# A spectral filter and an MLP on one core: the second DFT stage in quarters of the array, and VectorE's DFT operations spread over steps

## The chip, the cores and the metric

The kernel runs on one core of a Trainium2 chip. The metric is the device time of one execution in microseconds. Before the change three runs gave 776.87, 777.8 and 780.51, with a median of 777.8 us.

## What is computed

```python
X = np.fft.rfft(x, axis=1)                   # x: 8 x 3008 x 256
y = np.fft.irfft(X * (filt_r + 1j * filt_i), n=3008, axis=1)
h = y.reshape(24064, 256) @ w_in             # 256 x 2048
s = np.sin(alpha * h)
out = (h + s * s / (alpha + 1e-9)) @ w_out   # 2048 x 256
```

Eight batches pass through a Fourier filter along the sequence, and each of the 24064 rows through an MLP with a sine activation.

## The kernel before

**Two kinds of work share the engines.** The MLP is cut into 48 chunks (`chunks`, L588), twelve for each pair of batches, of 512 rows and one in twelve of 384; a chunk is eight *steps* (L749 to L760), so a batch is 48 steps. In each step `hidden` (L594) makes two blocks: two matmuls into a PSUM tile ph of the pool hps (L601), a cosine on ScalarE (L605), and on VectorE v, which reads the cosine and ph again (L606). `project` (L610) multiplies the v of the chunk before with w_out, eight matmuls a step (L620), and stores through ScalarE and a DMA queue. A ph tile is free once its v is made; hps has four buffers, so the blocks of a step reuse those of two steps ago.

**The DFT of the batches is slipped between the steps.** 3008 = 47 x 64. For a batch there are four stages, with a trip through DRAM after the first and after the third:
- first stage: 47 points over the columns. Batch 1 uses `first` (L203, 16 matmuls with the full table wf), later batches `first_tiled` (L214), whose eight matmuls per quarter of the batch use 64x64 quarters of the array: two row groups hold two different sets of x rows, two column groups two sets of n2. The results t1_h go to DRAM as d1 (L211, L229).
- second stage forward: `forward` (L238), 12 times a batch, two frequencies each, 128x128 tables d. `load_t2` (L233) reads d1 back on POOL's queue. ScalarE copies the PSUM to xf (L246), and two DMAs on SP's queue put its halves, exchanged, into xs.
- product with the filter: `product` (L253) multiplies xf into p, `cross` (L261) multiplies xs in place and adds it to p. xf and xs have three buffers, p seven.
- second stage inverse: `inverse` for batch 1 (L266), `inverse_tiled` later (L284): three bursts a batch of 16 quarter matmuls, evacuated into g by three ScalarE copies and one VectorE copy; g goes to DRAM as d2. `load_t4` and `last` (L316) finish into y, which the MLP reads.

Bursts use PSUM tiles of two pools: their first half (q = 0) takes the two of fps, their second half (q = 1) two of the four of hps, out of the same rotation as ph. Batch 0 has a path of its own ahead of the steps (L459 to L513).

**What sets the order.** Nothing is scheduled at run time: every engine works its instructions in the order in which the program issues them, and so do the DMA queues of SP and POOL. `put(at, fn)` (L671) gives each piece of the DFT a time in steps; `slot` (L735) issues the pieces due, once after the hidden blocks of a step and once after its projection. `firsts` and `inverses` (L674, L679) hold the times of the bursts; `clear` moves forwards off them, and `aside` (L689) moves a VectorE operation that would come just ahead of a burst to just behind it. `after` (L99) makes one instruction wait for another.

Of the kernel before, what the change touches and what calls it, by code (L numbers as in the profile page):

```python
# [24 lines left out]
FUSED = 1  # L25
TILED = 2


def dft_tables():
# [22 lines left out]
    f16 = np.float16  # L52
    wf, wi = wf.reshape(N1 * 2, 2, NS, 2), 2 * wi.reshape(2, NS, 2, NR)
# [13 lines left out]
    return (eh.astype(f16), wh.reshape(NK, NR).astype(f16), wt.reshape(128, 64).astype(f16), wf.transpose(0, 2, 1, 3).reshape(NR, NK).astype(f16), wi.reshape(NK, NR).astype(f16), d,  # L67
# [4 lines left out]
def kernel(  # L72
# [11 lines left out]
    eh_host, wh_host, wt_host, wf_host, wi_host, d_host, wf0_host, wi0_host, e_host = dft_tables()  # L84
# [3 lines left out]
    wf_dram = nc.inline_tensor(wf_host, name="wf_tbl")  # L88
    wi_dram = nc.inline_tensor(wi_host, name="wi_tbl")
# [20 lines left out]
    t2pool = pool("t2", 4)  # L110
    xfpool = pool("xf", 3)
    ppool = pool("pp", 7)
    xspool = pool("xs", 3)
# [8 lines left out]
    wf_t = cpool.tile([NR, NK], FP16)  # L122
# [22 lines left out]
    eh_t = e_t[:, 0:NS // 2].rearrange("p a (b m) -> p (a b) m", m=64)  # L145
# [3 lines left out]
    wi_t = cpool.tile([NK, NR], FP16)  # L149
    wi0_t = cpool.tile([128, NR], FP16)  # L150
    filt_t = cpool.tile([128, 2, NS, C], FP16)
    f_t = [filt_t[:, k] for k in range(2)]
# [3 lines left out]
    def load_x(b, ch):  # L156
        xt = xpool.tile([128, 8, C], FP16, name=f"x_{b}_{ch}", tag="x")
        if b >= TILED:
            for h in range(2):
                ins = nc.gpsimd.dma_start(  # L160
                    out=xt[64 * h:64 * h + N1],
                    in_=bass.AP(tensor=x.tensor, offset=x.offset + (b * S + 32 * h + ch * 8) * C,
                                ap=[[64 * C, N1], [1, 8 * C]]))
                after(ins, marks["snake"])
            return xt
        xt = xt[0:NR]
        for n0, n in [(0, 8)] if b or ch < 3 else [(0, 4), (4, 4)]:
            ins = nc.gpsimd.dma_start(
                out=xt[:, n0:n0 + n],
                in_=bass.AP(tensor=x.tensor, offset=x.offset + (b * S + ch * 8 + n0) * C,  # L170
                            ap=[[32 * C, NR], [C, n], [1, C]]),
            )
        if b == 0:
            marks["x", ch] = ins
        if b == 1:
            marks["x1", ch] = ins
            after(ins, marks["w_in"])
        return xt
# [3 lines left out]
    def evac(dst, src, on_act=None):  # L182
        flip[0] = (flip[0] + 1) % 3
        if flip[0] if on_act is None else on_act:
            marks["act"] = nc.scalar.copy(out=dst, in_=src)  # L185
        else:
            marks["dve"] = nc.vector.tensor_copy(out=dst, in_=src)  # L187

    class Spectral:

        def __init__(self, b):
# [3 lines left out]
            self.d1_rows = self.d1.rearrange("a (h n) c -> (a h) n c", h=2)  # L195
            self.d2_rows = self.d2.rearrange("a (h n) c -> (a h) n c", h=2)
            self.x, self.t2, self.t4, self.xf, self.xs, self.p = {}, {}, {}, {}, {}, {}
            self.fused = b >= FUSED

# [3 lines left out]
        def first(self, i):  # L203
            ch, j = divmod(i, 4)
            ps = fps.tile([128, 512], FP32, name=f"pa_{self.b}_{i}", tag="f")
            marks["pe"] = nc.tensor.matmul(out=ps[0:NK, :], lhsT=wf_t, rhs=self.x[ch][:, 2 * j:2 * j + 2, :],
                                           start=True, stop=True)
            r0 = 8 * (ch % 2)
            evac(t1_h[ch // 2][0:NK, r0 + 2 * j:r0 + 2 * j + 2, :], ps[0:NK, :])
            if j == 3:  # L210
                nc.sync.dma_start(out=self.d1_rows[:, 8 * ch:8 * ch + 8, :],   # L211
                                  in_=t1_h[ch // 2][0:NK, r0:r0 + 8, :])

        def first_tiled(self, ch):  # L214
            r0 = 8 * (ch % 2)
            for q in range(2):
                own, tag = (hps, "h") if q else (fps, "f")
                ps = [own.tile([128, 512], FP32, name=f"pa_{self.b}_{ch}_{q}_{h}", tag=tag) for h in range(2)]
                for h in range(2):
                    for c in range(2):  # L220
                        n = 4 * c + 2 * q
                        nc.tensor.matmul(out=ps[h][64 * c:64 * c + 64, :], lhsT=wt_t[64 * h:64 * h + N1],  # L222
                                         rhs=self.x[ch][64 * h:64 * h + N1, n:n + 2, :], start=True, stop=True)
                for h in range(2):
                    evac(t1_h[ch // 2][:, r0 + 4 * h + 2 * q:r0 + 4 * h + 2 * q + 2, :], ps[h], h == 0)
            d1 = self.d1.rearrange("a (h n) c -> a h (n c)", h=2)
            for c in range(2):
                n0 = (8 * ch + 4 * c) * C
                nc.sync.dma_start(out=d1[:, :, n0:n0 + 4 * C],  # L229
                                  in_=t1_h[ch // 2][64 * c:64 * c + 2 * NS, r0:r0 + 8, :]  # L230
                                  .rearrange("a (h n) c -> a h (n c)", h=2))

        def load_t2(self, g):  # L233
            self.t2[g] = t2pool.tile([128, 6, C], FP16, name=f"t2_{self.b}_{g}", tag="t2")
            nc.gpsimd.dma_start(out=self.t2[g], in_=self.d1[12 * g:12 * g + 12, :, :]  # L235
                                .rearrange("(s k) n c -> (k n) s c", k=2))

        def forward(self, u):  # L238
            b = self.b
            ps = fps.tile([128, 2, C], FP32, name=f"pb_{b}_{u}", tag="f")  # L240
            for i in range(2):
                s = 2 * u + i
                nc.tensor.matmul(out=ps[:, i, :], lhsT=d_t[:, s, :],  # L243
                                 rhs=self.t2[s // 6][:, s % 6, :], start=True, stop=True)
            self.xf[u] = xfpool.tile([128, 2, C], FP16, name=f"xf_{b}_{u}", tag="xf")
            nc.scalar.copy(out=self.xf[u], in_=ps)  # L246
            if self.fused:
                self.xs[u] = xspool.tile([128, 2, C], FP16, name=f"xs_{b}_{u}", tag="xs")
                for p in range(2):
                    nc.sync.dma_start(out=self.xs[u][64 * p:64 * p + 64, :, :],  # L250
                                      in_=self.xf[u][64 - 64 * p:128 - 64 * p, :, :])

        def product(self, u):  # L253
            self.p[u] = []
            for k in range(1 if self.fused else 2):
                pt = ppool.tile([128, 2, C], FP16, name=f"p_{self.b}_{u}_{k}", tag="p")
                marks["prod", u] = nc.vector.tensor_tensor(out=pt, in0=self.xf[u],  # L257
                                                           in1=f_t[k][:, 2 * u:2 * u + 2, :], op=ALU.mult)
                self.p[u].append(pt)

        def cross(self, u):  # L261
            xs, p = self.xs[u], self.p[u][0]
            nc.vector.tensor_tensor(out=xs, in0=xs, in1=f_t[1][:, 2 * u:2 * u + 2, :], op=ALU.mult)  # L263
            nc.vector.tensor_tensor(out=p, in0=p, in1=xs, op=ALU.add)  # L264

        def inverse(self, w):  # L266
            b = self.b
            pr = self.p.pop(w)
            if w % 3 == 0:
                self.g = gpool.tile([128, 6, C], FP16, name=f"g_{b}_{w}", tag="g")  # L270
            ps = fps.tile([128, 2, C], FP32, name=f"pc_{b}_{w}", tag="f")
            for i in range(2):
                for k, pt in enumerate(pr):
                    nc.tensor.matmul(out=ps[:, i, :], lhsT=e_t[:, 2 * w + i, :],
                                     rhs=pt[:, i, :], start=(k == 0), stop=(k == len(pr) - 1))
            i0 = 2 * (w % 3)
            evac(self.g[:, i0:i0 + 2, :], ps, True if b == 1 else None)
            if w % 3 == 2:
                for p in range(2):
                    a0 = p * NS + 6 * (w // 3)  # L280
                    nc.sync.dma_start(out=self.d2[a0:a0 + 6, :, :].rearrange("s n c -> n s c"),
                                      in_=self.g[64 * p:64 * p + 64, :, :])

        def inverse_tiled(self, w):  # L284
            g = gpool.tile([128, 4, 2, C], FP16, name=f"gt_{self.b}_{w}", tag="g")
            for q in range(2):
                own, tag = (hps, "h") if q else (fps, "f")
                ps = [own.tile([128, 2, C], FP32, name=f"pc_{self.b}_{w}_{q}_{k}", tag=tag) for k in range(2)]
                for i in range(2):
                    for k in range(2):  # L290
                        for c in range(2):
                            u = 4 * w + 2 * c + q
                            nc.tensor.matmul(out=ps[k][64 * c:64 * c + 64, i, :],  # L293
                                             lhsT=eh_t[64 * k:64 * k + 64, 2 * u + i, :],
                                             rhs=self.p[u][0][64 * k:64 * k + 64, i, :], start=True, stop=True)
# [3 lines left out]
            for c in range(2):  # L299
                z0 = 16 * w + 8 * c  # L300
# [491 lines left out]
```

## Time and profile before

| | |
|---|---|
| profiled execution | 779.97 us |
| span from its first to its last instruction | 778.2 us |
| TensorE matmul busy | 763.9 us (98%), granted clock 0.997 |
| VectorE busy | 658.2 us (85%) |
| ScalarE busy | 610.5 us (78%) |
| POOL busy | 371.2 us (48%) |
| first stage, quarter bursts (L222) | 192 matmuls, 15.0 us |
| second stage forward (L243) | 168 matmuls, 32.1 us |
| second stage inverse, quarter bursts (L293) | 288 matmuls, 11.6 us |
| DMA moved | 101.49 MB, mean 130 GB/s |

Busy time of matmuls overlaps from one to the next, since they are pipelined, and their ends are modelled; what a matmul costs is the distance from its start to the next one's. A group's line names the program's line, the engine, the operation, output and inputs, their shapes and the count; then busy time and mean duration, and after the bar the engine's idle time just before and what ended most of it. In a timeline the columns are start, length, engine, line, operation and count, and in brackets the idle time before with what ended it.

### The profile page before, as it was taken

The page shows a single profiled execution, that of the slowest core. Times are in us where ns is not written, and L with a number is a line of the kernel's source. Part 1 is how long each engine was busy: PE and PEld are TensorE (multiplying, and loading weights), DVE is VectorE, ACT ScalarE, POOL GpSimd, SP SyncE. Part 2 cuts the span into 40 slices and gives each one's busy share as a digit, 9 for nine tenths or more (in the row PEclk, how much of TensorE's full clock was granted, in tenths as well). Part 3 has the DMA queues.
Part 4 walks back from the last instruction along what each step waited for, and adds up shares of the span by engine and source line. Part 5 has one row for each costly group of instructions (what it writes and reads, how often), then busy time and mean ns, then how long its engine had stood idle before and what let it go on. Part 6 is the DMA issues. An engine that isn't in the chain of part 4 may idle for free.

```text
span 778.2 us, 17224 instructions
## 1 busy us (share of the span) xinstructions
PE 763.9 (98%) x6039; PEld 517.3 (66%) x6039; DVE 658.2 (85%) x1173; ACT 610.5 (78%) x1203; POOL 371.2 (48%) x649
## 2 busy tenths in 40 slices
PE   8999999999999999999999999999999999999997
PEld 4757766666666666666666666766666666766665
DVE  6986998999988888898889988899888888787773
ACT  5798888898888877888878787788778787777762
POOL 6355554634555655455464647554464655430000
PEclk9999999999999999999999999999999999999999
DMA  9955578854765428644474536764254332411112
GB/s 227 264 110 158 119 179 240 223 137 124 188 164 133 124 58 215 157 108 128 108 202 111 141 93 147 198 150 121 72 145 111 85 72 56 135 46 34 36 41 56
DMA packets 81518, 101.49 MB, mean 130 GB/s; under 512 B 18884, under 2 KB 60864, under 8 KB 81431
## 3 DMA queue, kind: packets, MB, share of 16 engines
q0 software_dynamic: 27440, 47.29, 25.9%
q1 hardware_dynamic: 53434, 52.79, 25.3%
q8 instruction: 47, 0.77, 0.4%
q10 hardware_dynamic: 557, 0.31, 0.2%
q14 instruction: 40, 0.33, 0.1%
HBM read 56.15 MB, written 46.66 MB: 132 GB/s over the span
## 4 chain that ended last, share of the span: by engine, by line
PE 91%; DVE 4%; DMA 2%; ACT 1%; issue 1%; ACTq 0%; POOLq 0%; DVEq 0%
PE po L620 40%; PE ph L601 40%; DVE v L606 3%; PE pd L316 2%; PE pb L243 2%; PE pa L222 2%; PE pc L293 1%; PE pc L513 1%; DMA w<-in_moe_alpha_dram 1%; PE warm L437 1%; DMA d<-t_h 1%; ACT cos_all L605 1%; PE pb L491 1%; DMA t<-d 1%; PE pa L459 1%
## 5 line engine op out<-in xcount | busy, mean ns | idle before, releaser
L606 DVE SCALAR_TENSOR_TENSOR v<-cos_all,ph 128x512 f16<-128x512 f32 (+1 forms) x768 | 482.7, 671 | 96.9 <-ACT cos_all L605 93.1
L605 ACT ACTIVATE cos_all<-ph 128x512 f32<-128x512 f32 (+1 forms) x768 | 413.7, 599 | 100.3 <-PE ph L601 99.8
L665 POOL DMA_DIRECT2D out_dram<-o x530 | 292.5, 558 | 241.8 <-ACT o L630 212.6
L601 PE MATMUL ph<-y,w 128*128 128x512 f16 (+1 forms) x1536 | 389.1, 375 | 1.3 <-DVE v L606 1.1
L620 PE MATMUL po<-w,v 128*128 128x256 f16 x3008 | 389.3, 273 | 0.0
L620 PEld LDWEIGHTS <-v 128*128 128x128 f16 x3008 | 290.1, 98 | 84.2 <-issue 1.1
L601 PEld LDWEIGHTS <-w 128*128 128x128 f16 x1536 | 143.2, 98 | 113.9 <-issue 19.0
L630 ACT COPY o<-po 128x512 f32<-128x512 f32 x94 | 55.9, 595 | 7.6 <-PE po L620 7.3
L246 ACT CAST xf<-pb 128x512 f16<-128x512 f32 x84 | 50.9, 606 | 2.2 <-PE pb L243 1.4
L185 ACT CAST y<-pd 128x376 f16<-128x376 f32 (+1 forms) x86 | 41.9, 490 | 12.2 <-PE pd L316 8.8
L160 POOL DMA_DIRECT2D x<-in_x_dram x48 | 25.6, 539 | 40.5 <-DVE v L606 26.7
L185 ACT CAST t_h<-pa 128x512 f16<-128x512 f32 (+1 forms) x60 | 32.8, 589 | 12.5 <-PE pa L222 11.3
L316 PEld LDWEIGHTS <-t_a 96*128 96x128 f16 x448 | 31.4, 97 | 12.7
L264 DVE TENSOR_TENSOR p<-p,xs 128x512 f16<-128x512 f16 x84 | 35.7, 425 | 2.9
L263 DVE TENSOR_TENSOR xs<-xs,filt_t 128x512 f16<-128x512 f16 x84 | 35.1, 418 | 1.6 <-DMA xs<-xf 1.5
L257 DVE TENSOR_TENSOR p<-xf,filt_t 128x512 f16<-128x512 f16 x84 | 35.0, 418 | 0.0
L185 ACT CAST gt<-pc 128x512 f16<-128x512 f32 x54 | 28.1, 594 | 8.4 <-PE pc L293 8.4
L187 DVE CAST t_h<-pa 128x512 f16<-128x512 f32 (+1 forms) x52 | 33.5, 682 | 0.2
L243 PE MATMUL pb<-t,d_t 128*128 128x256 f16 x168 | 32.1, 273 | 0.8 <-DMA t<-d 0.8
L316 PE MATMUL pd<-wh_t,t_a 96*128 96x94 f16 x384 | 31.8, 204 | 0.0
L235 POOL DMA_DIRECT2D t<-d x28 | 24.4, 873 | 13.2 <-DMA d<-t_h 11.2
L243 PEld LDWEIGHTS <-d_t 128*128 128x128 f16 x168 | 16.3, 98 | 15.3 <-DMA t<-d 1.0
(70 smaller groups left out, 277.9 us busy)
## 6 DMA issues: line engine op xcount, KB each, us to landing
t<-d POOLq DMA_DIRECT2D x28, 384.0 KB, 5.2
xs<-xf SPq DMA_DIRECT2D x168, 64.0 KB
t_a<-d SPq DMA_DIRECT2D x28, 384.0 KB
x<-in_x_dram POOLq DMA_DIRECT2D x50, 188.0 KB, 4.4
d<-t_h SPq DMA_DIRECT2D x48, 192.0 KB
d<-gt SPq DMA_DIRECT2D x36, 256.0 KB
out_dram<-o POOLq DMA_DIRECT2D x91, 64.0 KB, 2.1
out_dram<-o POOLq DMA_DIRECT2D x31, 80.0 KB, 3.8
```

The costliest lines, as they stand in the source:

```text
L185: marks["act"] = nc.scalar.copy(out=dst, in_=src)
L243: nc.tensor.matmul(out=ps[:, i, :], lhsT=d_t[:, s, :], rhs=self.t2[s // 6][:, s % 6, :], start=True, stop=True)
L246: nc.scalar.copy(out=self.xf[u], in_=ps)
L263: nc.vector.tensor_tensor(out=xs, in0=xs, in1=f_t[1][:, 2 * u:2 * u + 2, :], op=ALU.mult)
L264: nc.vector.tensor_tensor(out=p, in0=p, in1=xs, op=ALU.add)
L316: nc.tensor.matmul(out=psv[:, i, :], rhs=wi_t if self.b < TILED else wh_t, start=True, stop=True, lhsT=t4_h[ch // 2][0:NK, n0 % 16 + i, cb ...
L601: nc.tensor.matmul(out=ps[:, 0:n], lhsT=w1[:, cb, jb * 128:jb * 128 + 128], rhs=y_cols[:, cb, c0:c0 + n], start=(cb == 0), stop=(cb == 1))
L605: nc.scalar.activation(out=cs[:, 0:n], in_=ps[:, 0:n], func=AFT.Sin, bias=float(np.pi / 2))
L606: marks["snake"] = nc.vector.scalar_tensor_tensor(out=v[k][:, jb, 0:n], in0=cs[:, 0:n], scalar=-1.0, in1=ps[:, 0:n], op0=ALU.add, op1=ALU. ...
L620: nc.tensor.matmul(out=pso[k][:, t % 2, :], lhsT=v[k][:, jb, 128 * t:128 * t + 128], rhs=w2[:, jb, :], start=(jb == 0), stop=(jb == 15))
L630: copy(out=o[:, i0:t % 2 + 1, :], in_=pso[k][:, i0:t % 2 + 1, :])
L665: queues[i % len(queues)].dma_start(out=bass.AP(tensor=out.tensor, offset=out.offset + t0 * C, ap=[*ap, [1, C]]), in_=o_blk[p0:p0 + rows, :])
```

## The change

The forward second stage is done on sums and differences. The rows n2 and 63 - n2 are mirrored about the middle, so the 64-point sums split into a part over n2 + mirror and one over n2 - mirror, each of 32. Concretely:

- Batch 1 takes the same path as batches 2 to 7 (`TILED = 1`); `first`, `forward` and `inverse` in their full-array form go, and their tables wf and wi.
- `first` loads the second half of the rows in descending blocks and multiplies them in reverse, one row block of 256 at a time (six matmuls per half burst, of which four are half as long). Three of its four tiles are copied by ScalarE (two before).
- `mirror`, new, twice per `first`: VectorE adds (or subtracts) the two halves of t1_h[0] into t1_h[1], 128 x 1024, and two DMAs on SP's queue write 48 rows of 2 KB to d1.
- `forward`, three times a batch: 16 quarter matmuls of 256 columns with the table dh, four PSUM tiles, all four copied to xf by ScalarE, and the exchange to xs by two DMAs of 64 x 4 KB.
- `product`, `cross`, `add`: each on 128 x 1024, twice per forward, each with a time of its own. xf and xs are single tiles, p is two (one of them laid over e).
- `load_t2` reads two halves of 64 partitions per forward.
- The half tables dh and eh are laid over d, and loaded at step 3 instead of eh at step 54.
- The times in `firsts`, `forwards`, `inverses` are new, and `aside` reaches 0.6 step ahead of a burst instead of 1.1.

```diff
-FUSED = 1
-TILED = 2
+HS = NS // 2
+TILED = 1
...
-    eh_t = e_t[:, 0:NS // 2].rearrange("p a (b m) -> p (a b) m", m=64)
+    eh_t = d_t[:, 0:HS].rearrange("p a (b m) -> p (a b) m", m=64)
+    dh_t = d_t[:, HS:NS].rearrange("p a (k q) -> p a k q", k=2)
+    xf_t, xs_t, p_t = [cpool.tile([128, 2, 4, C], FP16, name=name) for name in ("xf_t", "xs_t", "p_t")]
...
+        def first(self, ch):
+            r0 = 8 * (ch % 2)
+            x = self.x[ch]
             for q in range(2):
                 own, tag = (hps, "h") if q else (fps, "f")
                 ps = [own.tile([128, 512], FP32, name=f"pa_{self.b}_{ch}_{q}_{h}", tag=tag) for h in range(2)]
+                for c in range(2):
+                    n = 4 * c + 2 * q
+                    nc.tensor.matmul(out=ps[0][64 * c:64 * c + 64, :], lhsT=wt_t[0:N1],
+                                     rhs=x[0:N1, n:n + 2, :], start=True, stop=True)
+                for i in range(2):
+                    for c in range(2):
+                        n = 4 * c + 2 * q + i
+                        nc.tensor.matmul(out=ps[1][64 * c:64 * c + 64, C * i:C * i + C], lhsT=wt_t[64:64 + N1],
+                                         rhs=x[64:64 + N1, 7 - n, :], start=True, stop=True)
                 for h in range(2):
+                    evac(t1_h[0][:, r0 + 4 * h + 2 * q:r0 + 4 * h + 2 * q + 2, :], ps[h], (q, h) != (1, 1))
+
+        def mirror(self, ch, e):
+            r0 = 8 * (ch % 2)
+            rows = self.d1.rearrange("(s k) (e j) c -> s k e (j c)", k=2, e=2)
+            part = t1_h[1][:, r0 + 4 * e:r0 + 4 * e + 4, :]
+            nc.vector.tensor_tensor(out=part, in0=t1_h[0][:, r0:r0 + 4, :], in1=t1_h[0][:, r0 + 4:r0 + 8, :],
+                                    op=ALU.subtract if e else ALU.add)
+            for c in range(2):
+                n0 = (8 * ch + 4 * c) * C
+                nc.sync.dma_start(out=rows[:, ::1 - 2 * e, e, n0:n0 + 4 * C],
+                                  in_=part[64 * c:64 * c + 2 * NS].rearrange("a n c -> a (n c)"))
+
+        def forward(self, w):
+            for q in range(2):
+                own, tag = (hps, "h") if q else (fps, "f")
+                ps = [own.tile([128, 2, C], FP32, name=f"pb_{self.b}_{w}_{q}_{a}", tag=tag) for a in range(2)]
+                for i in range(2):
+                    s = 2 * q + i
+                    for a in range(2):
+                        for k in range(2):
+                            nc.tensor.matmul(out=ps[a][64 * k:64 * k + 64, i, :],
+                                             lhsT=dh_t[64 * a:64 * a + 64, 4 * w + s, k, :],
+                                             rhs=self.t2[w][64 * a:64 * a + 64, 2 * s + k, :], start=True, stop=True)
+                for a in range(2):
+                    evac(xf_t[:, a, 2 * q:2 * q + 2, :], ps[a], True)
+            for p in range(2):
+                nc.sync.dma_start(out=xs_t[64 * p:64 * p + 64], in_=xf_t[64 - 64 * p:128 - 64 * p])
...
     def firsts(b):
 
-        return {2: (37.5, 39.5, 41.5, 43.5), 3: (49.5, 54.5, 60.5, 66.5)}.get(
-            b, [48 * b - 105.5 + 8 * ch for ch in range(4)])
+        return {1: (7, 8.5, 10, 11.5), 2: (37.5, 39.5, 41.5, 43.5), 3: (47.5, 56.5, 66, 76)}.get(
+            b, [48 * b - 98.5 + 8 * ch for ch in range(4)])
+
+    def forwards(b):
+
+        return {1: (17.5, 23.5, 29.5), 2: (51.5, 61, 70.5)}.get(b, [48 * b - 54.5 + 16 * w for w in range(3)])
 
     def inverses(b):
 
-        return (63.5, 73.5, 81.5) if b == 2 else [48 * b - 46.5 + 16 * w for w in range(3)]
+        return {1: (26.5, 32, 36), 2: (59.5, 69, 78.5)}.get(b, [48 * b - 46.5 + 16 * w for w in range(3)])
...
     def aside(at):
 
-        return next((s + 0.05 for s in bursts if s - 1.1 < at <= s), at)
+        return next((s + 0.05 for s in bursts if s - 0.6 < at <= s), at)
...
+        for ch in range(4):
+            at = firsts(b)[ch]
+            put(at, s.first, ch, pe=True)
+            for e in range(2):
+                put(aside(at + e + (1 if b < 3 else 5 if b > 3 and ch % 2 == 0 else 1.5)), s.mirror, ch, e)
+        for w in range(3):
+            fwd = forwards(b)[w]
+            put(14 if b == 1 else 46.5 if b == 2 else max(81, 48 * b - 68) if w == 0 else fwd - 16, s.load_t2, w)
+            put(fwd, s.forward, w, pe=True)
+            for a in range(2):
+                put(aside(fwd + (1 if b == 1 else 1.5) + a), s.product, w, a)
+                at = fwd + (3 + 1.5 * a if b == 1 else 4 + 2 * a)
+                put(aside(at), s.cross, w, a)
+                put(aside(at + (0.5 if b == 1 else 1)), s.add, w, a)
+            put(inverses(b)[w], s.inverse, w, pe=True)
```

## The prediction

> **What bounds the kernel now.** I read the chain that ended last first, then the costliest groups.
>
> ```profile
> PE 91%; DVE 4%; DMA 2%; ACT 1%; issue 1%; ACTq 0%; POOLq 0%; DVEq 0%
> ...
> L606 DVE SCALAR_TENSOR_TENSOR v<-cos_all,ph 128x512 f16<-128x512 f32 (+1 forms) x768 | 482.7, 671 | 96.9 <-ACT cos_all L605 93.1
> ...
> L243 PE MATMUL pb<-t,d_t 128*128 128x256 f16 x168 | 32.1, 273 | 0.8 <-DMA t<-d 0.8
> ```
>
> The chain is TensorE for 91% of the span. VectorE is busy 85% of it, and its 97 us of idle are waits for ScalarE's cosine: it keeps up, but with little room. How well TensorE is packed shows in its timeline around one step (a step: two hidden blocks, 4 matmuls of L601, and a projection of 8 of L620).
>
> ```profile
> 351.46 1.03 PE L601 MATMUL ph<-y,w 128*128 128x512 f16 x4
> 352.32 1.04 PE L620 MATMUL po<-w,v 128*128 128x256 f16 x8
> 353.29 0.63 PE L293 MATMUL pc<-p,e_t 64*64 64x256 f16 x16
> 353.86 1.04 PE L601 MATMUL ph<-y,w 128*128 128x512 f16 x4
> ```
>
> Durations overlap, so starts count. L601 takes 0.86 us for 4 (0.216 each) and the eight of L620, by their start-to-start, 8 x 0.109 = 0.87; a plain step is 1.74 us. The quarter-array burst of 16 then takes 353.86 - 352.32 - 0.87 = 0.67 us, 0.10 of it a gap ahead. Summing such spacings over the trace, steps 38 to 383 run within 2 us of the matmuls' own time. So every matmul saved is time saved, and every wait put on TensorE is time lost.
>
> Where the room ends shows in the one place where an inverse burst of batch 2 met a busy VectorE.
>
> ```profile
> 182.94 0.42 DVE L263 TENSOR_TENSOR xs<-xs,filt_t 128x512 f16<-128x512 f16 x1
> 183.39 0.42 DVE L264 TENSOR_TENSOR p<-p,xs 128x512 f16<-128x512 f16 x1
> 183.73 0.42 DVE L257 TENSOR_TENSOR p<-xf,filt_t 128x512 f16<-128x512 f16 x1
> 184.07 1.27 DVE L606 SCALAR_TENSOR_TENSOR v<-cos_all,ph 128x512 f16<-128x512 f32 x2
> ...
> ```
>
> ```profile
> 183.98 0.63 PE L293 MATMUL pc<-p,e_t 64*64 64x256 f16 x16
> 184.80 1.19 PE L601 MATMUL ph<-y,w 128*128 128x512 f16 x4 [0.18 <-DVE v L606]
> ```
>
> A burst takes two of the four hidden PSUM tiles, so the next hidden blocks need tiles whose v was made in the same step. Three VectorE operations (1.13 us) stood ahead of that step's two v; it began about 0.6 us late, and TensorE lost 0.24 us here. At 353.86, with nothing ahead, the second block found its tile free 0.29 us early. So **a burst forgives about 0.25 us of VectorE lateness and passes the rest on**; without a burst the tile is wanted a step later and 1.0 us passes unseen.
>
> **Removed from TensorE.** Forward: in each third of a batch, 8 matmuls x 0.109 = 0.87 us become one 0.67 us burst (the row of L293, same shape and count): 21 x 0.20 = 4.3 us. Batch 1: its 16 first-stage matmuls (3.5 us) become four bursts of 0.66, -0.9; its inverse 24 x 0.109 become 3 x 0.67, -0.6. The first stage's mirrored half streams the same columns in 256 instead of 512; I take no change, bounds 0 and +1. Sum **-5.7 us**. TensorEngine Tiling (Array Packing), Theoretical Speedup, in the Trainium skill gives up to 2x per dimension of 64 or less, which would make the forward burst 0.44 us and the saving of that stage 9 us; the row of L293 says 0.67, and it decides.
>
> **VectorE's own work hardly changes.** Start to start, one v takes (4.87 - 0.68)/7 = 0.60, a 1024-wide fp16 operation 0.60 (below), a 512-wide one 0.34.
>
> ```profile
> 22.41 3.10 DVE L501 TENSOR_TENSOR p<-xf,filt_t 128x1024 f16<-128x1024 f16 x5
> ...
> 39.71 4.87 DVE L606 SCALAR_TENSOR_TENSOR v<-cos_all,ph 128x512 f16<-128x512 f32 x8 [1.10 <-ACT cos_all L605]
> ```
>
> Per batch: 36 products, crosses and adds of 512 (12 x (0.34 + 0.45 + 0.34) = 13.6 us) become 18 of 1024 (about 11); first-stage copies 8 become 4 (-2.4); 8 mirror operations come in (+4.9). Net about 0, near 79 us in some 90 us. What changes is the place: bursts per batch go from 7 to 10 (batch 1: 0 to 10), and in the eight steps between a forward and its inverse burst come six operations of 0.6. A step that holds one needs 1.2 + 0.6 = 1.8 us of VectorE against 1.74 of TensorE.
>
> **ScalarE adds lateness.** A forward burst's four tiles are all copied by ScalarE, ahead of the next step's cosines.
>
> ```profile
> 353.74 1.56 ACT L185 CAST gt<-pc 128x512 f16<-128x512 f32 x3 [0.56 <-PE pc L293]
> 355.18 2.31 ACT L605 ACTIVATE cos_all<-ph 128x512 f32<-128x512 f32 x4
> ```
>
> Normally a cosine starts 0.63 us after its hidden block (351.46 to 352.09); behind three copies it started 1.32 after (353.86 to 355.18), 0.7 late. A fourth (0.48) makes 1.15, and v follows. First-stage bursts go from two such copies to three.
>
> **The sum of lateness**, carried step by step in the new instruction order: add VectorE's operations, subtract the step's TensorE time, never below zero or below the cosine's lateness, and at a burst pass on what exceeds 0.25. One cycle of batch 5 (forward 185, batch 6's first-stage burst 189, inverse 193): after 185, 1.15 late; 186, 0.63; 187 (product and a y copy, 2.27 against 2.07) 0.83; 188, 0.74; burst 189 passes on 0.50; its three copies leave 0.67; 190 (cross and add, 2.42 against 2.24) 0.85; 191 (cross, y, 2.27 against 1.90) 1.21; 192 (1.81 against 1.74) 1.29; burst 193 passes on **1.04**. The add just ahead of the inverse is late by the same and is not counted twice. All steps: 8.8 us in 7 to 37, 8.0 in 38 to 80, 6.5 in 81 to 176, 8.0 in 177 to 272, 3.6 after: 34.9. The same sum on the kernel before gives 1.7 in steps 38 to 383, where the trace has 1.8. Net +33 with ScalarE; with VectorE's own work alone 17.6, net +17. It has been tested only on lateness under 0.8 us, so I take two thirds of 33, **+22**; bounds 0 and +33.
>
> PSUM Bottleneck, in the same page of the Trainium skill, warns that copies out of PSUM may become the limit once tiling speeds TensorE up and wants both engines on them; the 1.56 us of copies behind a 0.57 us burst agree.
>
> **The way through DRAM, batch 1 and 2.** Before, the last first-stage copy of batch 1 ended at 64.49 and the forward began 8.95 us later, 0.9 of it TensorE's loss.
>
> ```profile
> 64.50 4.33 DMA d<-t_h
> ...
> 69.43 3.97 DMA t<-d
> ```
>
> ```profile
> 73.44 0.39 PE L243 MATMUL pb<-t,d_t 128*128 128x256 f16 x2 [0.77 <-DMA t<-d]
> ```
>
> Now three mirror operations stand together ahead of step 13's v and the fourth behind them; that ends about T13 + 3.2 + 1.6 (T13: the step's start; 2.55 to its second v's end, 0.6, and the step's lateness). Then 4.3 write, 0.5, a second POOL issue (0.84, both row halves are loaded) and 4.0: T13 + 14.4. The forward burst of 17.5 is due at T13 + 9.5. Stall 4.9, less the 0.9 of before: **+4**; bounds +2.4 (the writes are a quarter as large) and +5. Batch 2: mirror ends T45 + 4, the same way takes 10 to 11 us (t there waited until 133.35 for a write issued by 128.5, then 4.0 to 6.2 to land), burst due at T45 + 12 plus 1 of stalls: **+1**, bounds 0 and +2.5. From batch 3 on more than 8 steps lie between.
>
> Hidden otherwise: the two half tables (384 KB each) are put in SP's queue at step 3, with the first batch-1 write at step 8 behind them; if late they would hold up that write, bounds 0 and +2, taken as 0. The exchange xs is a single buffer now, 2 x 256 KB; its cross comes 4 steps (7 us) after the forward, against 2 us of copies and about 4 to 6 of transfer (the 384 KB loads land in 3.8 to 7.5): 0.
>
> **Sum.** The profiled execution took 779.97 us (span 778.2, 1.8 around it), 2.2 above the median of 777.8. -5.7 + 22 + 4 + 1 = +21.3: profiled about 801, median **799**.
>
> **Rivals.**
> *VectorE's share alone.* ScalarE's copies fit in without moving the cosines (for it: ScalarE idles 100 us for hidden blocks; against: the 0.7 us delay at 355.18). Two thirds of 17 are 11, so -5.7 + 11 + 5 = +10: 788.
> *The cover holds: faster.* Place: the inverse bursts. If VectorE is never over 0.25 us late when they come, and the round trip of batch 1 is at its low bound, what is left is -5.7 + 2.4 = -3.3, with some of the 1.8 us of present stalls gone, -5: 773. It decides at lateness 0.25 us per burst. For it: 42 bursts of before cost 1 us in all. Against: those had at most three small operations just ahead.
> *The single buffers bind.* xf and xs have one buffer each: VectorE's cross waits for the exchange and TensorE behind it, 1 us in each of 21 forwards on top: 820. Against: the 7 us above.
> *Quarters not side by side.* 16 x 0.109 = 1.74 instead of 0.67 would add 22 us; the row of L293 speaks plainly against it.
>
> **How the numbers follow.** Forecast (790 to 813) 0.57; VectorE alone (782 to 790) 0.18; single buffers 0.06, quarters 0.03; cover holds 0.16, of which 0.09 faster by over 0.5% (3.9 us, about what a measurement of this kernel can tell) and 0.07 within. Slower 0.84. The range takes in the lateness bounds (+33, with +5 and -5.7: 810; DMA at its high bound 813) and VectorE's share alone: 782 to 814.
>
> **What the new profile would show.** Forward bursts of about 0.6 us by 16 matmuls; TensorE idle ahead of hidden blocks after inverse bursts, released by VectorE's v, near 1 us each, and ahead of the forward of batch 1 by t<-d, near 5 us; cosines 1.1 us late after forward bursts. If hidden blocks wait under 0.3 us after inverse bursts, the lateness sum is wrong, and the forecast with it.

## The result and the profile after

The changed kernel takes 814.58 us (median of four runs, 814.08 to 815.18), the kernel before 778.43 on the same chip: a ratio of 1.0463, 95% interval 1.0436 to 1.0490. That is 36 us slower, where +21 was forecast and the range ended at 814. The profiled execution took 814.08 us, its span is 812.3 (before 779.97 and 778.2). The granted clock was 0.997 in both profiled executions, so the difference is not one of clock.

From the page of the kernel after, the chain that ended last, then three groups:

```profile
PE 56%; DVE 27%; ACT 8%; DMA 4%; issue 3%; POOL 0%; ACTq 0%; SPq 0%; POOLq 0%; DVEq 0%
...
L582 DVE SCALAR_TENSOR_TENSOR v<-cos_all,ph 128x512 f16<-128x512 f32 (+1 forms) x768 | 481.6, 670 | 132.8 <-ACT cos_all L581 130.9
...
L577 PE MATMUL ph<-y,w 128*128 128x512 f16 (+1 forms) x1536 | 396.0, 375 | 9.0 <-DVE v L582 6.3
...
L256 DVE TENSOR_TENSOR xs_t<-xs_t,filt_t 128x1024 f16<-128x1024 f16 x42 | 28.6, 682 | 0.1
```

The chain was 91% TensorE; now 27% of it runs through VectorE and 8% through ScalarE, because it crosses over at every stall. VectorE's amount of work has hardly moved (658.2 to 661.6 us, 85% to 81% of the span), while its waits for cosines grew from 93.1 to 130.9 us. It is not short of time on the whole; it is late at certain places. The last line says that the cross hardly ever waits for the exchange of xf (0.1 us idle ahead of all 42).

TensorE's waits in the kernel after (total, times, longest, in us):

```profile
PE ph L577 <- DVE v L582: 6.3, 14, 1.5
PE pb L241 <- DMA t<-d: 5.2, 4, 3.0
PE pc L271 <- DVE p_t L260: 4.3, 7, 1.1
PE pc L271 <- DVE e_t L260: 4.0, 7, 0.9
PE ph L577 <- ACT xf_t L181: 1.8, 2, 1.6
```

The third and fourth (p lies in two tiles, p_t and e_t) are one thing: an inverse burst waits for the add that makes its input. Before, the inverse bursts (L293) had no such row.

**A table of lost time** makes the kernels comparable. For each step: start-to-start of its first hidden block and the next step's, less its matmuls' own spacings (0.216 per hidden matmul, 0.109 per projection matmul, 0.67 per burst, and so on). Totals in us by steps, each from that kernel's profiled execution:

| kernel | 0–6 | 7–37 | 38–80 | 81–176 | 177–272 | 273–383 | sum |
|---|---|---|---|---|---|---|---|
| before | 2.1 | 3.1 | 0.8 | 0.6 | 0.5 | 0.0 | 7.0 |
| after | 2.1 | 14.9 | 10.1 | 8.2 | 10.4 | 3.5 | 49.1 |
| forecast for after, full lateness and waits | | 13.7 | 9.0 | 6.5 | 8.0 | 3.6 | 40.8 |
| e1, inverse bursts later | 2.1 | 15.0 | 9.6 | 6.6 | 8.0 | 0.8 | 42.0 |
| e2, copies shared | 2.1 | 14.3 | 9.1 | 7.2 | 8.7 | 1.0 | 42.4 |
| e12, forward copies narrow | 2.1 | 13.3 | 8.8 | 7.2 | 8.7 | 0.8 | 40.9 |
| e13, e1 and e2 | 2.1 | 15.2 | 9.7 | 5.9 | 6.6 | 0.0 | 39.5 |
| e3, filter narrow | 2.2 | 10.4 | 6.0 | 2.3 | 3.0 | 0.0 | 23.8 |
| e4, mirror narrow | 2.2 | 14.0 | 7.4 | 7.5 | 10.2 | 3.4 | 44.7 |
| e7, before with late crosses | 2.1 | 2.2 | 0.8 | 6.8 | 7.1 | 3.9 | 22.9 |
| e8, before with batch 1 in quarters | 2.2 | 7.1 | 1.2 | 0.6 | 1.4 | 0.0 | 12.3 |

So 42.1 us more are lost (49.1 less 7.0) and 5.7 saved by shorter matmul work: +36.4. Step 0 starts 2.2 us earlier in the span (36.2 against 38.4), which leaves +34.2; the spans differ by 34.1. That start lies between 36.0 and 38.7 us in the kernels of this study, and no edit explains it, so a single profiled execution carries some 2 us that have nothing to do with the steps.

### The profile page after: what moved, and what is told of

It reads as the page before. It is cut to its first block, busy times and chain, and to the rows that moved or that the text cites. A ratio compares the mean times of both kernels' runs of the same rounds, so it can differ in the third digit from the quotient of the medians.

```text
span 812.3 us, 17630 instructions
## 1 busy us (share of the span) xinstructions
PE 775.8 (96%) x6359; PEld 514.5 (63%) x6359; DVE 661.6 (81%) x1086; ACT 621.7 (77%) x1220; POOL 382.8 (47%) x670
## 4 chain that ended last, share of the span: by engine, by line
PE 56%; DVE 27%; ACT 8%; DMA 4%; issue 3%; POOL 0%; ACTq 0%; SPq 0%; POOLq 0%; DVEq 0%
PE ph L577 25%; PE po L596 24%; DVE v L582 17%; ACT cos_all L581 3%; DVE xs_t L256 3%; ACT xf_t L181 2%; ACT t_h L181 2%; DVE e_t L260 2%; DVE p_t L260 2%; PE pd L294 1%; DMA w<-id 1%; PE pc L271 1%; DVE t_h L219 1%; PE pb L241 1%; DMA t<-d 1%
## 5 line engine op out<-in xcount | busy, mean ns | idle before, releaser
L582 DVE SCALAR_TENSOR_TENSOR v<-cos_all,ph 128x512 f16<-128x512 f32 (+1 forms) x768 | 481.6, 670 | 132.8 <-ACT cos_all L581 130.9
L577 PE MATMUL ph<-y,w 128*128 128x512 f16 (+1 forms) x1536 | 396.0, 375 | 9.0 <-DVE v L582 6.3
L181 ACT CAST xf_t<-pb 128x512 f16<-128x512 f32 x84 | 43.1, 602 | 15.7 <-PE pb L241 15.7
L181 ACT CAST t_h<-pa 128x512 f16<-128x512 f32 x84 | 44.1, 600 | 12.2 <-PE pa L210 7.3
L181 ACT CAST g<-pc 128x512 f16<-128x512 f32 x63 | 32.9, 596 | 22.0 <-PE pc L271 21.4
L181 ACT CAST y<-pd 128x376 f16<-128x376 f32 (+1 forms) x82 | 40.8, 498 | 7.9 <-PE pd L381 3.9
L161 POOL DMA_DIRECT2D x<-in_x_dram x56 | 30.0, 540 | 27.6 <-PE ph L577 10.2
L219 DVE TENSOR_TENSOR t_h<-t_h 128x1024 f16<-128x1024 f16 x56 | 37.7, 682 | 0.0
L256 DVE TENSOR_TENSOR xs_t<-xs_t,filt_t 128x1024 f16<-128x1024 f16 x42 | 28.6, 682 | 0.1
L183 DVE CAST y<-pd 128x376 f16<-128x376 f32 (+2 forms) x46 | 24.8, 541 | 1.0 <-PE pd L381 1.0
L271 PEld LDWEIGHTS <-d_t 64*64 64x64 f16 x336 | 9.4, 105 | 18.0 <-issue 17.9
L183 DVE CAST t_h<-pa 128x512 f16<-128x512 f32 x28 | 19.1, 682 | 1.0 <-PE pa L210 1.0
L210 PE MATMUL pa<-x,wt_t 47*64 47x256 f16 x224 | 18.0, 274 | 1.8 <-ACT t_h L181 0.7
```

What stands on the lines that cost most here:

```text
L219: nc.vector.tensor_tensor(out=part, in0=t1_h[0][:, r0:r0 + 4, :], in1=t1_h[0][:, r0 + 4:r0 + 8, :], op=ALU.subtract if e else ALU.add)
L256: nc.vector.tensor_tensor(out=xs_t[:, a], in0=xs_t[:, a], in1=f_t[1][:, a, 4 * w:4 * w + 4, :], op=ALU.mult)
L577: nc.tensor.matmul(out=ps[:, 0:n], lhsT=w1[:, cb, jb * 128:jb * 128 + 128], rhs=y_cols[:, cb, c0:c0 + n], start=(cb == 0), stop=(cb == 1))
L582: marks["snake"] = nc.vector.scalar_tensor_tensor(out=v[k][:, jb, 0:n], in0=cs[:, 0:n], scalar=-1.0, in1=ps[:, 0:n], op0=ALU.add, op1=ALU. ...
```

## The experiments

Three theories stood. **A**, the forecast's: VectorE's and ScalarE's lateness meets bursts that forgive little. **B**: VectorE's own work alone, with ScalarE's copies harmless. **C**: the single buffers and the ways through DMA. Unless said otherwise the edit is to the kernel after; each time is compared with the kernel before on the same chip (777.6 to 778.9 us).

### Inverse bursts a step or two later (e1)

```diff
-    ... [48 * b - 46.5 + 16 * w for w in range(3)])
+    ... [48 * b - 44.5 + 16 * w - (w == 2) for w in range(3)])
```

> The changed kernel with the inverse bursts of batches 3 to 7 two steps later (the last of each batch one step later); nothing else moves. Theory A (VectorE and ScalarE lateness meets the bursts, 814.6 us now, about 40 us of TensorE waits): the sum of lateness for steps 81 to 383 falls from 18.1 to 13.2 us, so about 809 us, and waits inside the inverse bursts (11 us now in those steps) nearly go. Theory B (VectorE's own work alone counts, ScalarE's copies do not): 8.1 falls to 3.8, about 810, but then the waits at first-stage bursts shortly after a forward burst should be small. Theory C (the exchange through DMA and the single buffers): no change, 814.6.

807.75 us, 1.0376 (1.0346 to 1.0406). TensorE's waits for the add, in the kernel after 8.3 us in 14 times, come down to two, the one shown and 0.9 us for e_t, both in batch 2, where nothing was moved:

```profile
PE ph L577 <- DVE v L582: 8.5, 20, 1.5
...
PE pc L271 <- DVE p_t L260: 1.1, 1, 1.1
```

From the bursts that were moved the wait is gone, but a part of it comes back as waits of hidden blocks (6.3 to 8.5): VectorE is still late, only now the burst's input is not. C's 814.6 does not hold; A's 809 and B's 810 lie too close together to be told apart by this run.

### Two of the forward's four copies on VectorE (e2), and copies of 8 of 256 channels (e12)

```diff
-                    evac(xf_t[:, a, 2 * q:2 * q + 2, :], ps[a], True)
+                    evac(xf_t[:, a, 2 * q:2 * q + 2, :], ps[a], a == 0)
```

> The changed kernel with two of the four copies behind each forward burst on VectorE instead of ScalarE. VectorE gets 42 x 0.60 = 25 us more work, ScalarE 42 x 0.48 = 20 us less. Theory A: the cosine lateness of 1.15 us after a forward burst falls to about 0.2, the sum of lateness for all steps from 34.8 to 30.8, about 810 us. Theory B: VectorE's own sum stays at 17.6 to 17.9, so no gain, 814 to 816. Theory C: 814.6.

808.58 us, 1.0385 (1.0357 to 1.0413). VectorE got 42 copies more, its page line is

```profile
L183 DVE CAST xf_t<-pb 128x512 f16<-128x512 f32 x42 | 27.0, 684 | 4.3 <-PE pb L241 4.2
```

and the kernel became 6 us faster with 27 us more on the engine that was late. B falls here.

```diff
-                    evac(xf_t[:, a, 2 * q:2 * q + 2, :], ps[a], True)
+                    evac(xf_t[:, a, 2 * q:2 * q + 2, 0:8], ps[a][:, :, 0:8], True)
```

> The four ScalarE copies behind each forward burst take 8 of 256 channels (the rest of xf is left as it was); VectorE's work, the exchange and every wait stay. Theory A: the cosines behind a forward burst are no longer late, and the sum of lateness falls from 34.8 to 29.6: about 809 us. Theory B (VectorE's own work alone): 814.6. If ScalarE's delay were the main cause, most of the 36 us would go: 785.

806.32 us, 1.0349 (1.0327 to 1.0371): copies of 8 channels give 8 us, hardly more than sharing them. From step 81 on the two kernels lose the same (7.2, 8.7 and about 0.9). So the forward's copies on ScalarE cost 7 to 8 of the 42 us, and not most of it, which would have given 785.

### The filter's operations (e3) and the mirrors (e4) on 8 of 256 channels

```diff
-            nc.vector.tensor_tensor(out=xs_t[:, a], in0=xs_t[:, a], in1=f_t[1][:, a, 4 * w:4 * w + 4, :], op=ALU.mult)
+            nc.vector.tensor_tensor(out=xs_t[:, a, :, 0:8], in0=xs_t[:, a, :, 0:8], in1=f_t[1][:, a, 4 * w:4 * w + 4, 0:8], op=ALU.mult)
```

(product and add likewise, and p_t[0] is set to zero once at the start)

> Product, cross and add of batches 1 to 7 on 8 of 256 channels (the filter is left out for the other 248); every wait, DMA and copy stays. It takes about 0.53 us from each of 126 VectorE operations. Theory A: the sum of lateness falls from 34.8 to 11.2, about 791 us, and with the trace's somewhat larger sum down to 787. Theory B: 17.6 falls to 4.0, about 801 us. Theory C: the crosses still wait for the exchange, so 812 to 815.

792.28 us, 1.0169 (1.0140 to 1.0199), just above A's 787 to 791, and far from B's 801 and C's 812 to 815. An inverse burst in this kernel's TensorE timeline starts and ends without a wait:

```profile
422.95 0.63 PE L271 MATMUL pc<-e_t,d_t 64*64 64x256 f16 x16
423.51 1.04 PE L578 MATMUL ph<-y,w 128*128 128x512 f16 x4
```

Lost time falls by 25.3 us, the largest single share.

```diff
-            nc.vector.tensor_tensor(out=part, in0=t1_h[0][:, r0:r0 + 4, :], in1=t1_h[0][:, r0 + 4:r0 + 8, :],
+            nc.vector.tensor_tensor(out=part[:, :, 0:8], in0=t1_h[0][:, r0:r0 + 4, 0:8], in1=t1_h[0][:, r0 + 4:r0 + 8, 0:8],
```

> The mirror's sums and differences on 8 of 256 channels (the rest of the second half table of the first stage is left as it was); all else stays. Takes about 0.53 us from each of 56 VectorE operations, 30 us of its work. Theory A: the sum of lateness falls from 34.8 to 29.0, most of it in steps 38 to 80 (8.0 to 4.0), and the read-back of batch 1 comes about 1.5 us sooner: about 807 us. Theory B: 17.6 to 12.7, about 808. If VectorE's total work set the time, as much as 30 us would go: 785.

810.47 us, 1.0399 (1.0368 to 1.0429): a miss of 3.5 us. Some 29 us of VectorE work went (56 operations, 0.68 us each in the kernel after, 0.17 here) and 4.4 us came back, 3.6 of them in steps 7 to 80. Steps 81 to 383 hold 32 of the mirrors and 90 of the filter's 126 operations, which shorten by the same 0.51 us. Of the 22.1 us lost there, the filter's operations, some 46 us of work, took 16.8 with them when they went, and the mirrors, some 16 us, took 1.0: about 0.37 us for each microsecond of work against 0.06. Place counts, not amount alone.

### The same operations at another place, in the kernel before (e7)

```diff
-                put(aside(fwd + (4 if b == 1 else 4.5)), s.cross, u)
+                put(inverses(b)[u // 4] - 1 if b > 2 and u % 4 > 1 else aside(fwd + (4 if b == 1 else 4.5)), s.cross, u)
```

> The kernel before the change (778.4 us) with the last two of every four crosses of batches 3 to 7 moved to one step ahead of the inverse burst that needs them: the same operations, the same bursts, only another place. If lateness at a burst beyond about 0.25 us is what costs (theories A and B), each of the 15 bursts loses 0.8 to 2.1 us: a sum of 17 against 0.6, about 795 us. If what counts is the amount of VectorE's work or the number of bursts, it stays at 778.4.

796.38 us, 1.0225 (1.0200 to 1.0250). Not one instruction was added to the kernel before; in batches 3 to 7 two of each four crosses moved to the step ahead of their inverse burst. Lateness at bursts foretold 795, the amount of work or the number of bursts 778.4. TensorE's waits in it:

```profile
PE pc L293 <- DVE p L264: 6.1, 17, 0.8
PE ph L601 <- DVE v L606: 3.6, 17, 0.6
```

The first did not exist in the kernel before, the second was 1.1 us. Half of the change's 36 us is had without the change.

### Batch 1 in quarters, in the kernel before (e8)

```diff
-TILED = 2
+TILED = 1
-        return {2: (37.5, 39.5, 41.5, 43.5), ...
+        return {1: (7, 8.5, 10, 11.5), 2: (37.5, 39.5, 41.5, 43.5), ...
-        return (63.5, 73.5, 81.5) if b == 2 else ...
+        return {1: (27.5, 32.5, 37.5), 2: (63.5, 73.5, 81.5)}.get(b, ...
```

(the half table at step 3, batch 1's rows loaded after w_in)

> The kernel before the change with one part of the change alone: batch 1's first stage and inverse in quarter-array bursts (first bursts at 7, 8.5, 10, 11.5, inverse at 27.5, 32.5, 37.5), its forward as it was, no mirror; the half table is loaded at step 3. TensorE saves 1.5 us. Theory A: seven more bursts in a stretch where VectorE has crosses of 0.8 us in most steps: a sum of lateness of 4.9 us more, so about 781.5 us. Theory B: 3.3 more, about 780. If bursts cost only their own 0.67 us: 777.

782.29 us, 1.0052 (1.0036 to 1.0069). Quarters for batch 1's first stage and inverse alone lose 4.0 us more in steps 7 to 37 than the kernel before, though their matmuls are 1.5 us shorter; over all steps it is 5.3 more, and 5.3 - 1.5 = 3.8 is the measured difference. No sums, no mirrors, no new trip: bursts in a stretch that had none.

### Batch 1's forward later (e5, e10)

```diff
-        return {1: (17.5, 23.5, 29.5), ...      # forwards
+        return {1: (20.5, 25, 29.5), ...
-        return {1: (26.5, 32, 36), ...          # inverses
+        return {1: (28, 32, 36), ...
```

> The changed kernel with batch 1's forward bursts at steps 20.5, 25 and 29.5 instead of 17.5, 23.5 and 29.5, and its first inverse at 28 instead of 26.5. If the way through DRAM is what TensorE waits for at step 17 (3.0 us for the first half of the read-back, 0.9 for the second, and 1 to 2 us of cosine lateness behind it), these 4 to 5 us go: about 810 us, and step 20's forward waits under 0.5 us. If the wait only moves with the forward (the exchange, the half tables), 814.6.

818.16 us, 1.0501 (1.0473 to 1.0528): a miss. `aside` put the last cross of the first third behind the next forward, so that it works on the next third's exchange and waits for it. VectorE's row of it:

```profile
DVE xs_t L256 <- DMA xs_t<-xf_t: 6.7, 2, 4.1
```

This run shows what one xs tile costs once it binds (up to 4.1 us a time). In the kernel after it does not bind: 0.1 us in all, and C's part on the exchange falls.

```diff
+        return {1: (20.5, 26.5, 32.5), ...      # forwards
+        return {1: (29.5, 35, 38), ...          # inverses
```

> The changed kernel with batch 1's forward bursts at steps 20.5, 26.5 and 32.5, six steps apart as in the changed kernel, and its inverse bursts at 29.5, 35 and 38, so that no cross comes behind the next forward's exchange any more. If TensorE's wait at step 17 is the way through DRAM, step 20 waits under 0.5 us for the read-back and 4 us go; the sum of lateness is the same (35.0 against 34.8): about 810.5 us. If the wait follows the forward: 814.6.

817.13 us, 1.0505 (1.0468 to 1.0541): a miss again, and a telling one. (Here the last add of a half of batch 1 comes behind the inverse burst that should use it, so that part of the cross terms is missing.) The forward no longer waits for its input, and steps 7 to 37 lose 9.5 us instead of 14.9. But steps 38 to 80 lose 16.2 instead of 10.1. VectorE's timeline of e10, then the SP queue's:

```profile
129.21 0.69 DVE L219 TENSOR_TENSOR t_h<-t_h 128x1024 f16<-128x1024 f16 x1
135.63 0.69 DVE L219 TENSOR_TENSOR t_h<-t_h 128x1024 f16<-128x1024 f16 x1 [5.73 <-DMA d<-t_h]
```

```profile
112.80 9.11 SPq L279 DMA_DIRECT2D d<-g  x4
125.88 1.26 SPq L284 DMA_DIRECT2D t_a<-d  x3
127.24 12.98 SPq L223 DMA_DIRECT2D d<-t_h  x11
```

Batch 2's mirror must not overwrite a part of t1_h whose write to d1 (L223) is still under way. That write stood in SP's queue behind batch 1's loads of the last stage (L284), which went out only at 125.88, after the later inverse's writes. One wait of 5 us was exchanged for another of 6: neither of the two placements tried finds a spare step between batch 1's DRAM trip and batch 2's first stage.

### The repairs together (e9, e11, e13)

```diff
+                    evac(xf_t[:, a, 2 * q:2 * q + 2, :], ps[a], (q, a) != (1, 1))
```

(with the inverses of e1 and the batch 1 of e5)

> The changed kernel with three repairs at once: inverse bursts of batches 3 to 7 later as in the first experiment, one of the four copies behind a forward burst on VectorE, and batch 1's forwards later. Theory A: the sum of lateness falls from 34.8 to 27.2, the wait for DRAM of 4 us goes: about 802 us, still 24 us slower than the kernel before, since the ten bursts of a batch keep resetting the cosines by 0.7 to 1.15 us each. If the three causes were all there is to the loss, it would be near 778 or below.

809.25 us, 1.0386 (1.0359 to 1.0412), 7 us above A's 802, a miss: e5's cross behind the next forward, and its wait for the exchange, are in it too.

The next has the inverses of e1, the copies of e2 and the batch 1 of e10.

> Batch 1 as in the kernel beside it, the inverse bursts of batches 3 to 7 two steps later, and two of the four copies behind each forward burst on VectorE. Theory A: the sum of lateness 29.5 against 34.8, and 4 us of the way through DRAM: about 805 us, and as the two repairs alone each gave 1 to 2 us more than their sums, perhaps 802. If these three places were the whole loss: 780 or below.

806.13 us, 1.0351 (1.0326 to 1.0375), with e10's new wait in steps 38 to 80 (15.9 us lost). The last has e1 and e2 alone:

> The changed kernel with the two single repairs together and batch 1 left where it was: inverse bursts a step or two later, and two of the forward's four copies on VectorE. If the two recover different lateness (A: VectorE's filter operations ahead of the inverse burst, and ScalarE's copies behind the forward burst), the steps from 81 on lose 12 to 13 us instead of 22, steps 7 to 80 about 23 to 24 instead of 25, and the time is 803 to 805. If each only recovers what the other also would (B), about 807. Neither reaches the kernel before, since the opening stretch keeps some 20 us of loss above it.

805.19 us, 1.0329 (1.0302 to 1.0356), steps 81 to 383 lose 12.5 us: the first of the two cases, different lateness. Of the 6.8 and 5.2 us that e1 and e2 take from these steps, 9.6 of 12 add up. This is the best form of the changed kernel that was found, 26 us behind the kernel before, and 25 us of its loss lie in steps 7 to 80. There e1 moves nothing, and sharing the copies of batches 1 and 2, which alone took 25.0 to 23.4, gains next to nothing beside it (24.9; 23 to 24 was expected).

Beside the ways through DRAM and the step behind the first of them (1.8), the largest single losses of these steps in the kernel after lie between the forward bursts of steps 23 and 29 and the hidden blocks behind them: 1.65 and 1.94 us. A cross and an add of the third before stand ahead of the step's v on VectorE there, and ScalarE has the burst's four copies to make. In e3 nothing is lost at these two places, in e12 0.4 and 0.6: a forward burst meets lateness as an inverse burst does.

## Why the prediction went wrong, point by point

**Direction and mechanism were right.** Slower was given 0.84, for lateness meeting bursts, and the faster rival, a cover that holds, needed every inverse burst to meet a VectorE less than 0.25 us late: the add alone made them wait 8.3 us. The worked cycle can be laid beside the trace. TensorE of the kernel after, steps 189 and 193 of batch 5:

```profile
429.61 0.40 PE L205 MATMUL pa<-x,wt_t 47*64 47x512 f16 x2
429.86 0.38 PE L210 MATMUL pa<-x,wt_t 47*64 47x256 f16 x4
430.49 1.19 PE L577 MATMUL ph<-y,w 128*128 128x512 f16 x4 [0.26 <-DVE v L582]
...
437.87 0.29 PE L271 MATMUL pc<-e_t,d_t 64*64 64x256 f16 x1
438.86 0.63 PE L271 MATMUL pc<-e_t,d_t 64*64 64x256 f16 x15 [0.70 <-DVE e_t L260]
439.46 1.19 PE L577 MATMUL ph<-y,w 128*128 128x512 f16 x4
```

Step 189 lost 0.32 (forecast 0.50), step 193 1.02 (forecast 1.04), from 437.87 to 439.46 less the 0.57 that a burst takes. VectorE over the same time:

```profile
430.96 0.68 DVE L183 CAST t_h<-pa 128x512 f16<-128x512 f32 x1
432.15 1.28 DVE L582 SCALAR_TENSOR_TENSOR v<-cos_all,ph 128x512 f16<-128x512 f32 x2 [0.51 <-ACT cos_all L581]
433.35 0.68 DVE L256 TENSOR_TENSOR xs_t<-xs_t,filt_t 128x1024 f16<-128x1024 f16 x1
434.07 0.69 DVE L260 TENSOR_TENSOR e_t<-e_t,xs_t 128x1024 f16<-128x1024 f16 x1
434.68 1.28 DVE L582 SCALAR_TENSOR_TENSOR v<-cos_all,ph 128x512 f16<-128x512 f32 x2
435.88 0.54 DVE L183 CAST y<-pd 128x376 f16<-128x376 f32 x1
436.33 0.68 DVE L256 TENSOR_TENSOR xs_t<-xs_t,filt_t 128x1024 f16<-128x1024 f16 x1
436.93 1.27 DVE L582 SCALAR_TENSOR_TENSOR v<-cos_all,ph 128x512 f16<-128x512 f32 x2
438.13 0.68 DVE L260 TENSOR_TENSOR e_t<-e_t,xs_t 128x1024 f16<-128x1024 f16 x1
```

Behind the first-stage burst it waits for a cosine until 432.15, and from there it works without a gap to the end of the add at 438.81: 6.66 us, in which the burst, due at 437.87, cannot be met. In e12 the same chain begins with a wait until 427.71 and takes 6.67 us, although ScalarE's forward copies take 0.18 us each there instead of 0.60:

```profile
427.71 1.28 DVE L582 SCALAR_TENSOR_TENSOR v<-cos_all,ph 128x512 f16<-128x512 f32 x2 [1.13 <-ACT cos_all L581]
...
433.70 0.68 DVE L260 TENSOR_TENSOR e_t<-e_t,xs_t 128x1024 f16<-128x1024 f16 x1
```

Step 189 loses 0.00 and step 193 loses 1.50. So in this cycle, with a first-stage burst between, the forward's copies cost only at that burst, and what is not lost there is lost at the inverse. Four more cycles are alike: the inverse bursts of steps 113, 161, 209 and 257 lose 0.93, 0.39, 0.77 and 0.85, and in e12 1.50, 0.88, 1.04 and 1.50; three others (97, 145, 241) lose the same in both within 0.04. Where no first-stage burst lies between they do reach the inverse: steps 129, 177 and 225 lost 0.44, 0.74 and 0.57 us, in e12 0, 0 and 0.25, and the four inverse bursts of steps 273 to 383 lost 0.44, 1.02, 0.56 and 0.89 us, in e12 0, 0.28, 0 and 0.25. ScalarE's delay itself came as forecast; its timeline after the forward burst of step 185:

```profile
421.76 2.05 ACT L181 CAST xf_t<-pb 128x512 f16<-128x512 f32 x4 [0.56 <-PE pb L241]
423.67 1.13 ACT L581 ACTIVATE cos_all<-ph 128x512 f32<-128x512 f32 x2
```

The block began at 421.87, so its cosine came 1.80 us after it instead of 0.63: 1.17 late, forecast 1.15. PSUM Bottleneck, in TensorEngine Tiling (Array Packing) of the Trainium skill, advises both engines for such copies; e2 agrees, with -6 us.

**The step that failed is the discount: "It has been tested only on lateness under 0.8 us, so I take two thirds of 33, +22."** The table's third row is the sum as it was worked out, with the two DRAM stalls: 40.8 us against 49.1 measured less 2.1 at the start, 47.0. The step sum was not too large by a third; it was too small by 6 us. Taken whole, it gives -5.7 + 33 + 5 = +32, 810 us, and 814.6 was measured. In the terms of the forecast, lateness was put at +22 and came to some +37 (42.1 less 5 for the ways through DRAM). There was no row for the discount; a caution that one has no number for belongs into the range (where +33 stood, as a bound) and not into the value. What the sum lacked: the step behind a stalled burst loses 0.16 us more (steps 194, 274, 290, 306 and 322 among others); and a first-stage burst can wait for a tile of fps, as at step 197, just behind a pd of the last stage, which was forecast clean and lost 1.07. TensorE and VectorE there:

```profile
447.00 0.40 PE L205 MATMUL pa<-x,wt_t 47*64 47x512 f16 x2
448.09 0.30 PE L210 MATMUL pa<-x,wt_t 47*64 47x256 f16 x2 [0.68 <-ACT t_h L181]
```

```profile
444.98 2.57 DVE L582 SCALAR_TENSOR_TENSOR v<-cos_all,ph 128x512 f16<-128x512 f32 x4
447.47 0.54 DVE L183 CAST y<-pd 128x376 f16<-128x376 f32 x1
```

The copy of pd into y ends at 448.01, the first pa copy on ScalarE (named as releaser) at 448.03; either frees a tile of fps, and which one was waited for stays open. In e3, e4 and e12 the step loses the same 1.07, so neither the filter's operations, nor the mirrors, nor the forward's copies cause it.

**VectorE against ScalarE.** The working gave VectorE alone 17 of the 33 (it does not show what it took off 17.6; less the 1.7 that it gives for the kernel before, 16 are left). The runs give its filter operations 25 of 42 (e3), the forward's copies 8 (e12), the mirrors 4 (e4). These shares come from three edits, each on its own, and need not add up.

**TensorE's saving, -5.7, held**: an unstalled forward burst takes 421.87 - 420.34 - 0.87 = 0.66 us (its projection began at 420.34), so quarters do lie side by side and that rival is out. The 0.44 us worked out from Theoretical Speedup, in TensorEngine Tiling (Array Packing) of the Trainium skill, is not reached. The lost time and the saving together give the measured difference to about 1 us.

**The way through DRAM, +4, held.** VectorE, POOL and TensorE of the kernel after:

```profile
65.09 0.68 DVE L219 TENSOR_TENSOR t_h<-t_h 128x1024 f16<-128x1024 f16 x1
```

```profile
70.30 4.09 POOL L230 DMA_DIRECT2D t<-d  x6 [7.75 <-DMA d<-t_h]
```

```profile
74.08 0.30 PE L241 MATMUL pb<-t,d_t 64*64 64x256 f16 x2 [2.99 <-DMA t<-d]
75.29 0.62 PE L241 MATMUL pb<-t,d_t 64*64 64x256 f16 x14 [0.91 <-DMA t<-d]
```

From the last mirror's end (65.77) to the second half of t2 it took 9.5 us (forecast 9.6), and the step lost 4.2 (forecast stall 4.9). Batch 2's (step 51) lost 1.6, forecast 1. C holds for these two places, 5 to 6 us. Beside them TensorE waits for a DMA in one more step, 0.8 us at step 56 for rows of x.

**The half tables, the exchange and the mirrored first stage, each taken as 0**: the exchange is shown (0.1 us); for the other two no longer spacing is seen, nor a wait but for that 0.8 us, and they were not tried alone.

**One announced sign was misplaced.** Hidden blocks behind inverse bursts were to wait near 1 us. In steps 81 to 383 they and the other hidden blocks lost 5.8 us, behind each of the 15 inverse bursts some 0.2; 11.0 us are lost one place earlier, inside the burst, whose second matmul needs the add. Both are the same lateness; the add, issued behind the step's two v, has no 0.25 us of grace. By its letter the sign of a wrong sum, under 0.3 us behind inverse bursts, came true; it looked one place too late and does not refute the sum: the lateness it stood for is there, inside the burst.

## What to carry to other kernels

Where one engine sets the pace and another is 80 to 85% busy, count the second one's operations up to each consumer, in the order of issue: e7 lost 18 us by a move alone, and e4 took 29 us of work away and won 4. If such a count agrees with the few rows that exist, put the whole of it into the forecast. And a burst that shortens the pacing engine by 0.2 us is paid for by what it does to its neighbours: who copies it out, whose tiles it takes, and what must be ready when it starts.

## What the runs showed that was not expected

From step 81 on, VectorE's taking the forward's copies off ScalarE (42 of 0.68 us in all steps) cost nothing that can be seen: e2, where it does so, and e12, where ScalarE copies 8 channels instead, lose the same there (16.9 and 16.7 us). Lost time moves rather than vanishes: e12 saves 0.32 us at step 189 and loses 0.48 more at step 193. And the later forward of e10 showed that a load which waits in SP's queue holds up writes of another batch behind it, 5.7 us of VectorE's idle time.
